# Four moves in a fused attention and feed-forward kernel: x's last transposes, a pair of output banks, one step up, and four idle matmuls

## The chip, the cores and the metric

The kernel runs on one core of a Trainium2 chip. Five engines work side by side, each through its own list of instructions in order: PE (matrix products and transposes, which write the PSUM banks), ACT (exponentials, Relu, copies), DVE (vector arithmetic and copies), POOL (masking of tiles, and issuing of loads) and SP (issuing of transfers). They wait for one another by semaphores. The metric is the device time of one execution in microseconds (us); lower is better.

## The reference, cut to what matters

Two parts follow one another. The first is attention for 4 batches, 8 heads, 768 tokens and 64 dimensions, in which each query sees only 6 of the 24 chunks of 32 keys, chosen by an upper bound (`ub`) from each chunk's smallest and largest key:

```python
ub = np.sum(np.maximum(q[:, :, :, None, :] * k_min[:, :, None, :, :], q[:, :, :, None, :] * k_max[:, :, None, :, :]), axis=-1)
top_chunks = np.argsort(ub, axis=-1)[..., -top_k:]
scores = scale * np.matmul(q, k.transpose(0, 1, 3, 2))
mask = sel & (pos[:, None] >= pos[None, :])
attn = np.exp(scores)      # of the masked scores, then divided by the row's sum
```

The second part takes the attention's result as x (3072 tokens of 512) through a feed-forward layer with 2048 hidden units:

```python
h = np.maximum(x @ w_in, 0.0)
return (h * h @ w_out).astype(np.float32)
```

## The kernel before, in words

**Slots.** The attention's work is cut into 32 slots, counted from 0. A slot is one batch, one half of its 768 tokens (384 queries) and one pair of heads. Four slots (four pairs) make a half batch, called hb; the order of the half batches is (batch 0, first half), (batch 1, first half), (batch 0, second half), (batch 1, second half), and so on. So slots 0 to 3 are hb 0, slot 4 (the fifth pair) opens hb 1, slot 8 opens hb 2, and slot 12 (the thirteenth slot) opens hb 3.

**Steps of a slot.** Each is a function, written below with the slot's number:
- P(s) transposes k and q of a slot on PE (L274: `tk`, `tq`). ACT and DVE copy them into `kq` (L300), ACT also makes q's positive and negative parts `qr` (L295), and DVE the chunk extrema `km` and `kbd` (L237, L240). From slot 12 on `qr` is made by DVE from transposes that the DMA did (L323, L324).
- U(s) forms the bounds `ub` on PE (L378 to L389), and DVE picks the six largest (L396) and marks the rest (L398: `chosen`, `nsel`).
- V(s) transposes the marks on PE (`qt`, L431 or L442), and DVE copies them beside q (L436, L447), so that the scores' own product adds a large negative number to chunks that were not chosen.
- E(s,h,n) makes scores `ps` of head h, part n (L460, and L468 for the triangular mask in slots 0 to 3), and ACT their exponentials `e` (L471). From slot 4 on POOL masks the diagonal blocks (L475).
- F(s) multiplies `e` with the values (`po`, L493), for both heads, and DVE divides by the sums (L502, L503), which gives a part of x.

**The feed-forward queue.** When the four pairs of a half batch have given x, it is transposed, on PE for some parts (`x_T`, L531, copied to `xT` by ACT or DVE at L537) and by DMA for others (L507). `push(hb)` then puts the half batch's steps into a queue: 16 steps up (`ffn_up`, L579: four matmuls for 128 hidden units, then Relu on ACT at L585 or L589 and a square on DVE) and 12 steps down (`ffn_down`, L602: four matmuls of 512 columns; four such steps (t,0) to (t,3) make the tile t of 128 output rows, which is then copied to `ob` and stored). `f1()` takes one step from the queue, and the loop over the slots places f1 calls between the attention's steps, by hand, up to a quota for each slot. This order is the order of each engine's list; nothing reorders it.

**PSUM.** Eight banks in four pools, handed out in turn: psS (3: scores, and some q or k transposes), psF (2, tag "ph": results of the steps up, transposes of x, early transposes of k), psY (1, tag "py": a tile of steps down, and some transposes) and psA (2: bounds, marks, `po`, and the idle matmuls). A tile that takes a bank waits until its last reader is done.

**Idle matmuls.** `busy(n)` (L685) issues n products of the identity with itself whose result nobody reads.

Of the kernel before, what the change touches and what calls it, by code (L numbers as in the profile page):

```python
# [30 lines left out]
ON_PE = 3  # L31
# [8 lines left out]
def kernel(  # L40
# [9 lines left out]
    nc = tc.nc  # L50
# [309 lines left out]
    def step_P(s):  # L360
        if s // NP >= ON_PE:
            relus(s)
            return
        step_T(s, *((S_, Y) if s == NP + 1 else (F, Y) if s < NP + 2 else
                    (Y, S_) if s < 2 * NP + 1 else (S_, A)))
        if s >= NP + 2 and s != 2 * NP + 1:
            step_T2(s)
# [168 lines left out]
    def x_copy(hb, g, u0, u1, copy):  # L536
        copy(xT_of(hb)[:, 2 * g + u0:2 * g + u1, :], pts[hb, g][:, u0:u1, :])  # L537
# [14 lines left out]
    def ffn_downs(hb, tail=False):  # L552
        py = {}
        order = [(t, c) for t in range(HT - tail) for c in range(4)]
        if hb == 0:

            order = [(0, 0), (0, 1), (1, 0), (1, 1), (0, 2), (1, 2), (0, 3), (1, 3)] + order[8:]
        return [lambda act, t=t, c=c: ffn_down(hb, py, t, c, act, tail) for t, c in order]

    def ffn_last(hb):  # L560
# [31 lines left out]

    def ffn_down(hb, py, t, c, act, tail):
        if c == 0:
            if hb == 0 and t == 1:
                py[t] = psF.tile([128, DM], F32, tag="ph", name="py")
            elif tail:
                py[t] = psS.tile([128, DM], F32, tag="ps", name="py")
            else:
                py[t] = psY.tile([128, DM], F32, tag="py", name="py")  # L600
        for f in range(4 * c, 4 * c + 4):
            nc.tensor.matmul(  # L602
                py[t], lhsT=h2[hb, f][:, 128 * t:128 * (t + 1)], rhs=w_out[:, f, :],
                start=(f == 0), stop=(f == NFI - 1))
        if c == 3:
            ob = late.tile([128, DM], F32, tag="ob", bufs=3, name="ob")
            if act:
                nc.scalar.copy(ob, py[t])  # L608
            else:
                nc.vector.tensor_copy(ob, py[t])  # L610
            r0 = S * ORDER[hb][0] + HB * ORDER[hb][1] + 128 * t
            nc.sync.dma_start(out[r0:r0 + 128, :], ob)
# [68 lines left out]
    def busy(n, pool=psA, tag="att"):  # L681

        idle = pool.tile([128, 128], F32, tag=tag, name="idle")
        for _ in range(n):
            nc.tensor.matmul(idle, lhsT=ident, rhs=ident, start=True, stop=True)  # L685
# [32 lines left out]
    late = ctx.enter_context(tc.tile_pool(name="late", bufs=2))  # L718
    for s in range(NP):
        last = s + 1 == NP  # L720
        if last:
            busy(4)
        if s:
            step_E(s, 0, 0)
            if not last:

                step_T(s + 2, F, Y, "k")
                extrema(s + 2, 0)
            step_E(s, 0, 1)
        step_E(s, 1, 0)  # L730
        if last:
            step_F(s - 1, 0)
            step_F(s - 1, 1)
        step_U(s + 1)
        if not last:
            busy(3)
            extrema(s + 2, 1)
            place(s + 1, "k", nc.scalar.copy)
        step_E(s, 1, 1)
        if last:  # L740
            x_T(0, 0, F)
            x_copy(0, 0, 0, 2, nc.scalar.copy)
            place(s + 1, "q", nc.scalar.copy)
            place(s + 1, "k", nc.scalar.copy, 1, 2)
            step_F(s, 0)
            step_F(s, 1)
            step_V(s + 1)
        else:
            step_T(s + 2, F, Y, "q")
            relus_T(s + 2)  # L750
            step_V(s + 1)
            if s:
                step_F(s - 1, 0)
                step_F(s - 1, 1)
            extrema(s + 2, 2)
            if s + 2 == NP:
                place(s + 2, "k", nc.vector.tensor_copy, 0, 1)
        go(s, 99)
    parts = []

    def k1():
        if parts:
            parts.pop(0)()

    for s, (b, half, p) in enumerate(slots):
        if s < NP:
            continue
        hb = s // NP
        nb = len(BANKS[half])
        hf = nb // 2  # L770
        quota = [((5, 5, 4, 4) if hb == 1 else (8, 5, 6, 7) if hb == 2 else (8, 6, 7, 7))[p]]
        for fn, *a in first.get(s, ()):
            fn(*a)
        if (hb == ON_PE - 1 and p == 2) or (ON_PE < hb < 2 * B - 1 and p == 0):
            parts.extend(step_K(hb + 1))

        def f1():
            if quota[0] and queue:
                quota[0] -= 1
                fill(1, True)  # L780

        if s == NP:
            for n in range(hf):
                step_E(s, 0, n)
            step_P(s + 1)
            relus_T(s + 1)
            x_T(0, 1, F)
            x_copy(0, 1, 0, 2, nc.vector.tensor_copy)
            push(0)
            extrema(s + 1)  # L790
            place(s + 1, "k", nc.vector.tensor_copy)
            place(s + 1, "q", nc.scalar.copy)
        if s == 2 * NP:
            for n in range(hf):
                step_E(s, 0, n)
            relus_T(s + 1)
            place(s + 1, "q", nc.scalar.copy)
            step_F(s - 1, 0)
            step_F(s - 1, 1)
            f1()  # L800
            x_T(1, 1, F, (1,))
            f1()
            extrema(s + 1)
            place(s + 1, "k", nc.vector.tensor_copy)
            put_off()
            x_copy(1, 1, 1, 2, nc.vector.tensor_copy)
            push(1)
        if p == 0 and hb > 2:
            step_F(s - 1, 0)
            step_F(s - 1, 1)  # L810
            put_off()
            push(hb - 1)
        else:
            f1()
        if s > NP and s != 2 * NP:
            for n in range(hf):
                step_E(s, 0, n)
        k1()
        f1()
        if p == 0 and hb > 2:  # L820
            f1()
            f1()
        if hb > 1 and s != 2 * NP:
            f1()
        if hb < ON_PE:
            go(s, 4 if s == 2 * NP else 2)
        for n in range(hf, nb):
            step_E(s, 0, n)
        if hb < ON_PE and p:
            k1()  # L830
        if s < NS - 2 or s + 1 == 3 * NP:
            step_U(s + (1 if hb < ON_PE else 2))
        if s == NP:
            put_off()
        if s + 1 == ON_PE * NP:
            put_off(2)
        if hb >= ON_PE and s < NS - 2:
            step_W(s + 2)
        if s == 2 * NP:

            for x in nsel:
                nc.vector.memset(
                    x[:, :, :, :, 1, :].rearrange("p i h j c -> p (i h j) c"), 0.0)
        late_f = half == 0 and hb > 2
        border = p == 0 and hb > 1
        if not border and not (late_f and p == NP - 1) and s + 1 != 2 * NP:
            f1()
        if p and s > NP:
            step_F(s - 1, 0)
            step_F(s - 1, 1)  # L850
        for fn, *a in by_sp.get(s, ()):
            fn(*a)
        if s + 1 == ON_PE * NP:
            step_P(s + 2)
            step_Q(s + 2)
        if half == 0 and not (late_f and p in (0, NP - 1)):
            f1()
        if hb < ON_PE and p:
            k1()
        for n in range(hf):  # L860
            step_E(s, 1, n)
            if border and half and n == 0:

                f1()
        if not (late_f and p == 0):
            f1()
        if s + 1 <= ON_PE * NP:
            step_V(s + 1)
        if s + 1 == ON_PE * NP:
            put_off(2)  # L870
        if hb == ON_PE and p == 0:
            parts.extend(step_K(hb + 1))
        k1()
        if hb < ON_PE:
            go(s, 99)
        for n in range(hf, nb):
            step_E(s, 1, n)
        if hb >= ON_PE:
            go(s, 99)
        k1()  # L880
        if hb == ON_PE - 1 or (hb == ON_PE and p):
            k1()
        if s + 1 < ON_PE * NP:
            step_P(s + 2)
            if s + 2 == ON_PE * NP:
                step_Q(s + 2)
        if s + 1 == ON_PE * NP:
            f1()
            step_U(s + 2)
            step_W(s + 2)  # L890
        if hb >= ON_PE or s + 1 == ON_PE * NP:
            if s + 3 < NS:
                step_P(s + 3)
                step_Q(s + 3)
        f1()
        if half == 0:
            f1()
        while quota[0] and queue:
            f1()
# [40 lines left out]
```

## Time and profile before

| | us |
|---|---|
| median of 3 runs | 266.37 (266.06 to 266.40) |
| the profiled execution | 266.18 |
| its span in the profile | 264.5 |

| engine | busy us | share of the span |
|---|---|---|
| PE | 253.7 | 96% |
| ACT | 178.4 | 67% |
| DVE | 162.5 | 61% |
| POOL | 91.1 | 34% |

The span runs from the first to the last instruction in the profile; 1.7 us of the execution lie around it. A row of the timeline gives start, length, engine, line of the kernel, operation, output<-inputs, shape and count; in brackets stands how long the engine was idle ahead of it and what ended the wait. Rows merge neighbouring instructions of one kind. The printed end of a PE row is modelled and overlaps the start of the next, so that the difference of two starts is the better measure of what PE spent. The granted clock of TensorE (PEclk) is 1.00 throughout.

### The profile page before, as it was taken

The page shows a single profiled execution, that of the slowest core. Times are in us where ns is not written, and L with a number is a line of the kernel's source. Part 1 is how long each engine was busy: PE and PEld are TensorE (multiplying, and loading weights), DVE is VectorE, ACT ScalarE, POOL GpSimd, SP SyncE. Part 2 cuts the span into 40 slices and gives each one's busy share as a digit, 9 for nine tenths or more (in the row PEclk, how much of TensorE's full clock was granted, in tenths as well). Part 3 has the DMA queues.
Part 4 walks back from the last instruction along what each step waited for, and adds up shares of the span by engine and source line. Part 5 has one row for each costly group of instructions (what it writes and reads, how often), then busy time and mean ns, then how long its engine had stood idle before and what let it go on. Part 6 is the DMA issues. An engine that isn't in the chain of part 4 may idle for free.

```text
span 264.5 us, 6559 instructions
## 1 busy us (share of the span) xinstructions
PE 253.7 (96%) x2402; PEld 157.4 (60%) x2428; DVE 162.5 (61%) x619; ACT 178.4 (67%) x399; POOL 91.1 (34%) x134
## 2 busy tenths in 40 slices
PE   7897999999999999999999999999999999999995
PEld 6575665556666566655565566745565666645543
DVE  6787998867986568566875566555863233424411
ACT  4898997698974787844685778835685788614500
POOL 8966445607902435225521543310120111000000
PEclk9999999999999999999999999999999999999999
DMA  7999999999994899999995999995642220111022
GB/s 140 162 194 189 206 219 184 135 182 112 155 158 90 141 164 156 133 158 153 184 144 119 147 157 130 212 126 127 123 99 64 72 45 17 58 40 41 0 82 79
DMA packets 116161, 33.69 MB, mean 127 GB/s; under 512 B 102560, under 2 KB 112576, under 8 KB 116128
## 3 DMA queue, kind: packets, MB, share of 16 engines
q0 software_dynamic: 65200, 13.83, 66.6%
q1 hardware_dynamic: 49984, 19.03, 37.7%
q10 hardware_dynamic: 944, 0.39, 0.6%
q8 instruction: 19, 0.31, 0.5%
q14 instruction: 14, 0.11, 0.1%
HBM read 27.26 MB, written 6.29 MB: 127 GB/s over the span
## 4 chain that ended last, share of the span: by engine, by line
PE 77%; DVE 8%; ACT 3%; issue 2%; ACTq 0%; DVEq 0%
PE py L602 28%; PE ph L579 26%; PE ps L460 11%; PE po L493 7%; DVE km L343 2%; ACT e L471 2%; PE ub L382 1%; PE py L567 1%; DVE km L237 1%; DVE kq L447 1%; DVE h L590 1%; DVE kq L300 1%; ACT ht L589 1%; PE tk L274 0%; ACT ob L608 0%
## 5 line engine op out<-in xcount | busy, mean ns | idle before, releaser
L471 ACT ACTIVATE e<-ps 128x512 bf16<-128x512 f32 x192 | 96.7, 550 | 18.9 <-PE ps L460 17.6
L579 PE MATMUL ph<-xT,w_in 128*128 128x384 bf16 x512 | 98.9, 325 | 0.4 <-DVE xT L537 0.4
L602 PE MATMUL py<-w_out,h 128*128 128x512 bf16 x342 | 82.7, 379 | 2.2 <-DVE kq L300 0.3
L590 DVE TENSOR_TENSOR h<-ht 128x384 bf16<-128x384 bf16 x114 | 41.8, 376 | 55.4 <-ACT ht L589 54.8
L475 POOL TENSOR_SCALAR_AFFINE_SELECT e<-e 128x384 bf16<-128x384 bf16 x56 | 30.1, 537 | 129.0 <-ACT e L471 128.8
L589 ACT ACTIVATE ht<-ph 128x384 bf16<-128x384 f32 x114 | 55.5, 500 | 26.8 <-PE ph L579 26.4
L579 PEld LDWEIGHTS <-w_in 128*128 128x128 bf16 x512 | 47.8, 97 | 30.7 <-issue 1.5
L460 PE MATMUL ps<-kq 96*128 96x384 bf16 (+2 forms) x320 | 57.9, 278 | 2.2 <-DVE kq L436 1.3
L602 PEld LDWEIGHTS <-h 128*128 128x128 bf16 x368 | 34.6, 97 | 35.6 <-issue 0.6
L460 PEld LDWEIGHTS <-kq 96*128 96x128 bf16 x320 | 26.4, 97 | 17.0 <-issue 2.6
L493 PEld LDWEIGHTS <-e 128*128 128x128 bf16 x672 | 25.2, 98 | 4.1 <-DVE x L503 0.4
L493 PE MATMUL po<-vn,e 128*128 128x65 bf16 x672 | 26.6, 194 | 0.3 <-DVE x L503 0.3
L608 ACT COPY ob<-py 128x512 f32<-128x512 f32 x18 | 10.5, 586 | 22.6 <-PE py L602 22.2
L396 DVE MAX8 m<-ub 128x8 f32<-128x16 f32 (+4 forms) x160 | 16.1, 166 | 15.6 <-PE ub L389 9.4
L503 DVE TENSOR_TENSOR x<-po,r 128x384 bf16<-128x384 f32 x32 | 17.8, 557 | 1.1
L237 DVE TENSOR_REDUCE km<-tk 128x12 bf16<-128x384 bf16 x24 | 12.5, 550 | 1.7 <-PE tk L274 1.4
L109 POOL DMA_DIRECT2D kn<-in_k_dram x15 | 13.3, 897 | 0.4 <-issue 0.3
L109 POOL DMA_DIRECT2D qn<-in_q_dram x15 | 13.3, 896 | 0.2
L125 POOL DMA_DIRECT2D vn<-in_v_dram x15 | 12.5, 842 | 2.0 <-DMA qn<-in_q_dram 1.3
L343 DVE TENSOR_TENSOR km<-km 128x384 bf16<-128x384 bf16 (+3 forms) x40 | 12.0, 300 | 1.1
L382 PEld LDWEIGHTS <-qr 128*128 128x128 bf16 x160 | 7.8, 96 | 4.8 <-DVE qr L323 1.7
L382 PE MATMUL ub<-kbd,qr 128*128 128x48 bf16 (+1 forms) x160 | 9.7, 180 | 1.0 <-DVE qr L323 0.5
(79 smaller groups left out, 193.3 us busy)
## 6 DMA issues: line engine op xcount, KB each, us to landing
out_dram<-ob SPq DMA_DIRECT2D x23, 256.0 KB, 2.4
w_out<-in_moe_w_out_dram POOLq DMA_DIRECT2D x2, 1024.0 KB, 18.2
kn<-in_k_dram POOLq DMA_DIRECT2D x15, 128.0 KB, 6.1
qn<-in_q_dram POOLq DMA_DIRECT2D x15, 128.0 KB, 5.9
kq<-kqT SPq DMA_DIRECT2D x10, 192.0 KB, 4.6
vn<-in_v_dram POOLq DMA_DIRECT2D x4, 384.0 KB, 7.8
vn<-in_v_dram POOLq DMA_DIRECT2D x9, 128.0 KB, 8.3
w_in<-in_moe_w_in_dram POOLq DMA_DIRECT2D x2, 512.0 KB, 9.0
```

Source lines behind the costliest of these rows:

```text
L109: nc.gpsimd.dma_start(out=nat_of(n, g)[:, DM * j:DM * j + DM].rearrange("p (h d) -> p h d", d=D), in_=rows(n, *ORDER[g], 0, H)[:, 128 * j: ...
L343: nc.vector.tensor_tensor(y, x[:, :, :, 0:m], x[:, :, :, m:2 * m], op=op)
L382: nc.tensor.matmul(ub[:, j - j0], lhsT=st[s]["qr"][:, w, 128 * j:128 * (j + 1)], rhs=kbds[b % 2][:, p, w, :, 0:ncs], start=bool(half) and ...
L460: nc.tensor.matmul(ps[:, at:at + 128 * m], lhsT=kqs[b % 2][0:KR, p, 2 * (j // HT), hh, 128 * (j % HT):128 * (j % HT + 1)], rhs=qc(s, hh)[: ...
L471: nc.scalar.activation(e[:, 512 * n + lo:512 * n + hi], ps[:, lo:hi], ACT.Exp, scale=float(scale))
L475: nc.gpsimd.affine_select(out=d, in_=d, compare_op=ALU.is_ge, fill=0.0, base=0, channel_multiplier=-1, pattern=[[0, 3], [1, 128]])
L493: nc.tensor.matmul(po[:, hh, i, :], lhsT=t["e"][hh][:, c:c + 128], rhs=vn[b % 2][:, 2 * p + hh, j, :], start=(j == 0), stop=(j == iq))
L503: nc.vector.tensor_mul(x[:, p].rearrange("p j (h d) -> p h j d", h=2), po[:, :, :, 0:D], r.to_broadcast([128, 2, HT, D]))
L579: nc.tensor.matmul(ph[:, 0:HB], lhsT=w_in[:, ki, 128 * f:128 * (f + 1)], rhs=xT[:, ki, :], start=(ki == 0), stop=(ki == NKI - 1))
L589: nc.scalar.activation(ht, ph[:, 0:HB], ACT.Relu)
L590: nc.vector.tensor_mul(h, ht, ht)
L602: nc.tensor.matmul(py[t], lhsT=h2[hb, f][:, 128 * t:128 * (t + 1)], rhs=w_out[:, f, :], start=(f == 0), stop=(f == NFI - 1))
```

## The change

Four edits, none of which changes what is computed:

1. In the last slot of hb 0 (slot 3) the four idle matmuls go, and F(2) runs ahead of E(3,1,0) instead of behind it.
2. In slot 4, P(5) and the transposes of x's second half of hb 0 (pairs 2 and 3) with their copy run ahead of E(4,0,0) instead of behind it.
3. Of hb 0's steps down, tile 0 takes a bank of psF and tile 1 that of psY, where it was the other way round, and (1,3) runs ahead of (0,3).
4. In slot 11, one step up runs ahead of U(12), and the one behind U(12) goes.

On PE's list the idle matmuls (eight rows with their weight loads) are all that goes. On ACT's list, slot 5's `qr` (L295) stands ahead of the exponential of E(4,0,0), and the two copies of the output tiles change places. DVE, POOL and SP keep their lists, but for which of the two tiles a store belongs to.

```diff
-            order = [(0, 0), (0, 1), (1, 0), (1, 1), (0, 2), (1, 2), (0, 3), (1, 3)] + order[8:]
+            order = [(0, 0), (0, 1), (1, 0), (1, 1), (0, 2), (1, 2), (1, 3), (0, 3)] + order[8:]
...
     def ffn_down(hb, py, t, c, act, tail):
         if c == 0:
-            if hb == 0 and t == 1:
+            if hb == 0 and t == 0:
                 py[t] = psF.tile([128, DM], F32, tag="ph", name="py")
...
     for s in range(NP):
         last = s + 1 == NP
-        if last:
-            busy(4)
...
             step_E(s, 0, 1)
-        step_E(s, 1, 0)
         if last:
             step_F(s - 1, 0)
             step_F(s - 1, 1)
+        step_E(s, 1, 0)
         step_U(s + 1)
...
         if s == NP:
+            step_P(s + 1)
+            x_T(0, 1, F)
+            x_copy(0, 1, 0, 2, nc.vector.tensor_copy)
+            relus_T(s + 1)
             for n in range(hf):
                 step_E(s, 0, n)
-            step_P(s + 1)
-            relus_T(s + 1)
-            x_T(0, 1, F)
-            x_copy(0, 1, 0, 2, nc.vector.tensor_copy)
             push(0)
...
+        if s + 1 == ON_PE * NP:
+            f1()
         if s < NS - 2 or s + 1 == 3 * NP:
             step_U(s + (1 if hb < ON_PE else 2))
...
-        if not border and not (late_f and p == NP - 1) and s + 1 != 2 * NP:
+        if not border and not (late_f and p == NP - 1) and s + 1 not in (2 * NP, 3 * NP):
             f1()
```

## The prediction

> **What bounds the kernel.** I read the page's first part and its chain, then the windows, then what PE waited for, then the timeline engine by engine around the three places that the change touches.
>
> ```profile
> span 264.5 us, 6559 instructions
> ...
> PE 253.7 (96%) x2402; PEld 157.4 (60%) x2428; DVE 162.5 (61%) x619; ACT 178.4 (67%) x399; POOL 91.1 (34%) x134
> ...
> PE 77%; DVE 8%; ACT 3%; issue 2%; ACTq 0%; DVEq 0%
> ```
> ```profile
> core 0: us, PE busy (x) PEld busy (x) DVE busy (x) ACT busy (x) POOL busy (x), PEclk, DMA share, GB/s
> 20.00:30.00 10.00, 8.39 (x117) 5.64 (x116) 7.69 (x30) 8.77 (x21) 5.39 (x8) 1.00 1.51 196
> 30.00:44.00 14.00, 13.36 (x161) 8.64 (x156) 13.36 (x46) 12.89 (x33) 8.32 (x12) 1.00 1.27 209
> ...
> 84.00:120.00 36.00, 35.66 (x333) 22.04 (x336) 21.62 (x85) 24.90 (x54) 13.12 (x18) 1.00 1.33 146
> ```
> ```profile
> PE ps L460 <- DVE kq L447: 1.0, 1, 1.0
> ```
>
> PE is the bound: the chain is 77% PE, and from 84 to 120 us PE is idle for 36.00 - 35.66 = 0.34 us. From 20 to 30 us it is idle for 1.61 us, and the waits name its longest stop; the others stand in brackets in the rows below. A stop of PE that goes away in the first 84 us is time off the end, unless another engine or a transfer takes the stop's place. From 30 to 44 us DVE is as full as PE (13.36 of 14.00 us), so there both must move.
>
> **The opening, 19 to 27 us.** Slots count from 0, so the fifth pair is slot 4.
>
> ```profile
> 19.42 0.38 PE L685 MATMUL idle<-ident 128*128 128x128 bf16 x4 [0.27 <-DVE kq L436]
> 19.64 0.39 PE L460 MATMUL ps<-kq 96*128 96x384 bf16 x2
> ...
> 20.14 0.38 PE L460 MATMUL ps<-kq 96*128 96x384 bf16 x2
> ...
> 20.48 0.54 PE L493 MATMUL po<-vn,e 128*128 128x65 bf16 x12
> 20.85 0.18 PE L378 MATMUL ub<-cmask,ident 128*128 128x48 bf16 x1
> ...
> 22.44 0.30 PE L442 MATMUL qt<-ident,chosen 128*64 128x128 bf16 x2
> 23.72 0.38 PE L460 MATMUL ps<-kq 96*128 96x384 bf16 x2 [0.98 <-DVE kq L447]
> 24.03 0.37 PE L274 MATMUL tk<-ident,kn 96*64 96x96 bf16 x8
> 24.23 0.36 PE L274 MATMUL tq<-ident,qn 96*64 96x96 bf16 x8
> 24.52 0.51 PE L531 MATMUL pt<-ident,x 128*128 128x128 bf16 x6
> 24.87 0.49 PE L579 MATMUL ph<-xT,w_in 128*128 128x384 bf16 x2
> 25.73 1.14 PE L579 MATMUL ph<-xT,w_in 128*128 128x384 bf16 x6 [0.38 <-DVE xT L537]
> ...
> 26.98 1.46 PE L579 MATMUL ph<-xT,w_in 128*128 128x384 bf16 x8
> ```
> ```profile
> 20.23 1.64 ACT L471 ACTIVATE e<-ps 128x512 bf16<-128x512 f32 x4 [0.28 <-PE ps L468]
> 21.73 0.83 ACT L537 COPY xT<-pt 128x768 bf16<-128x768 bf16 x1
> 22.41 0.99 ACT L300 COPY kq<-tq 64x384 bf16<-64x384 bf16 x2
> ...
> 24.20 0.60 ACT L471 ACTIVATE e<-ps 128x512 bf16<-128x512 f32 x1 [0.42 <-PE ps L460]
> 24.69 0.65 ACT L295 ACTIVATE qr<-tq 128x256 bf16<-128x256 bf16 x2
> 25.22 0.96 ACT L300 COPY kq<-tq 64x384 bf16<-64x384 bf16 x2
> 26.26 0.49 ACT L585 ACTIVATE h<-ph 128x384 bf16<-128x384 f32 x1
> ```
>
> Starts of neighbouring rows give what a step takes on PE; the printed lengths overlap. The four idle matmuls take 19.64 - 19.42 = 0.22 us. They wait for the same DVE copy (L436) as the scores after them, so without them E(3,0,0) starts at 19.42. F(2) takes 20.85 - 20.48 = 0.37 us; it now runs ahead of E(3,1,0) and needs only exponentials of slot 2, which were finished before ACT went idle ahead of 20.23.
>
> What this does to ACT: the first exponential comes 20.23 - 19.64 = 0.59 us after its scores start. E(3,1,0) now starts at 19.42 + 0.50 (for E(3,0,0) and E(3,0,1), as from 19.64 to 20.14, where E(3,1,0) stood) + 0.37 = 20.29, and its exponential at 20.88. Half of the block (21.73 - 20.23 = 1.50) follows from there, so the xT copy starts at 21.63 instead of 21.73. ACT gains only 0.1 us.
>
> That matters, because slot 5's q transposes (tq) write the bank that ACT's two copies of slot 4's q (L300) must empty first. Before, the scores stood ahead of them and hid that; now the whole PE queue behind V(4) (tq, x's transposes, E(4,0,0), the steps up) waits for it. The copies end at 22.41 + 0.99 - 0.10 = 23.30, so tq can start at about 23.35. Then tq takes 0.29 (24.52 - 24.23) and x's transposes 0.35 (24.87 - 24.52): E(4,0,0) starts at 23.99, later than its 23.72 of before, takes 0.31, and the steps up start at 24.30 instead of 24.87. DVE's copies of slot 4's masks, which held E(4,0,0) for 0.98 us, are done by then: they follow V(4), which is no later than 22.44, and ended by 23.72 before.
>
> ```profile
> 29.87 0.36 DVE L590 TENSOR_TENSOR h<-ht 128x384 bf16<-128x384 bf16 x1 [0.28 <-ACT ht L589]
> ```
>
> The third matmul of the first step up waits for the copy of x's last transposes; it came 25.73 - 24.52 = 1.21 us after they started, so now at 23.64 + 1.21 = 24.85: 0.88 us earlier. But the third step up needs the bank of the first, which ACT empties after e(4,0,0) and the two q copies of slot 5. E(4,0,0) at 23.99 gives its exponential at 24.47 (0.48 later, as 24.20 to 23.72); with 0.49 until the next one starts (24.69 - 24.20) and 0.96 for the copies, the first step's Relu starts at about 25.92 and ends at 26.41, and the third step up starts at 26.46 instead of 26.98. I take this 0.52, not 0.88. The stretch from 30 us on is paced by DVE as well, but DVE enters it idle (0.28 us before 29.87, waiting for ACT on the fifth step up), so it moves with PE. Bounds: nothing if tq gets its bank 0.5 us later than 23.35, a loss beyond that; at most 1.0, if all of the stop at 23.72 goes.
>
> **The banks.**
>
> ```profile
> 43.77 1.04 PE L602 MATMUL py<-w_out,h 128*128 128x512 bf16 x3 [0.32 <-DVE kq L300]
> ```
> ```profile
> 42.93 0.49 ACT L585 ACTIVATE h<-ph 128x384 bf16<-128x384 f32 x1
> ```
>
> The first step down took the bank from which DVE still copied slot 8's k, and PE stopped for 0.32 us. It now takes a bank of the steps up, freed when ACT ends the fifteenth step's Relu at 42.93 + 0.49 = 43.42: it starts at 43.47, 0.30 earlier. Tile 1 takes the other bank three steps later, long after DVE's copy. Swapping (0,3) and (1,3), and with them their copies on ACT and their output DMAs on SP's queue, costs nothing: the tile in the bank that tile 2 needs still ends one step (four matmuls) ahead of tile 2's first. Bounds 0 (ACT late by 0.3) to 0.32.
>
> **The step up in slot 11.**
>
> ```profile
> 74.65 0.55 PE L460 MATMUL ps<-kq 96*128 96x128 bf16 x3
> 75.70 0.47 PE L382 MATMUL ub<-kbd,qr 128*128 128x48 bf16 x6 [0.50 <-DVE qr L323]
> 76.03 0.81 PE L579 MATMUL ph<-xT,w_in 128*128 128x384 bf16 x4
> 76.68 1.12 PE L493 MATMUL po<-vn,e 128*128 128x65 bf16 x30
> ```
> ```profile
> 74.56 0.89 ACT L585 ACTIVATE h<-ph 128x384 bf16<-128x384 f32 x2
> ```
>
> The scores end at 74.65 + 0.55 = 75.20, but printed ends overlap the next start by some 0.17 (24.03 + 0.37 against 24.23), so PE is free at about 75.03. The step up needs a bank that the first of the two Relus frees at 74.56 + 0.49 = 75.05 (0.49 by the row of 42.93). With 0.05 for the signal it runs from 75.10 for 76.68 - 76.03 = 0.65 us to 75.75. Then the bounds run without a stop, since qr was there at 75.70: they took 76.03 - 75.70 = 0.33 while the second half of qr came late; by their columns (seven matmuls of up to 48, where a transpose of 128 takes 0.058) 0.15 is enough, and I take 0.22. F(10) starts at 75.97 instead of 76.68: 0.71 less. Nobody waits longer for U(12): its result comes at 76.0 either way. Bounds: 0.50 (the stop alone) to 0.72; 0.33 if the bank comes only with the second Relu at 75.45.
>
> **Sum.** 0.52 + 0.30 + 0.71 = 1.53 us, against the profiled execution: 264.5 of span and 1.7 around it, 266.18; it is 0.2 below the runs' median of 266.37. 266.18 - 1.53 = 264.65, from the median 264.84; I say 264.8.
>
> Does a transfer take over? The nearest is the last half of w_in, which the ninth step up needs:
>
> ```profile
> 19.84 0.76 POOL L631 DMA_DIRECT2D w_in<-in_moe_w_in_dram  x1
> ```
> ```profile
> w_in<-in_moe_w_in_dram POOLq DMA_DIRECT2D x1, 1024.0 KB, 12.0
> ```
> ```profile
> 33.37 0.81 PE L579 MATMUL ph<-xT,w_in 128*128 128x384 bf16 x4
> ```
>
> It lands at 19.84 + 12.0 = 31.8; the step moves from 33.37 to 32.85. One microsecond is left.
>
> **Rivals.** (a) The opening gives nothing: tq's bank frees at 23.9 or later, or the third step up keeps waiting for ACT. For it: ACT is busy 8.77 of 10 us there, the stage's fullest engine. Then 0.30 + 0.71 = 1.01: 265.3. (b) ACT keeps up and 0.88 to 1.0 arrives: about 1.95, 264.4. (c) The edits move PE but the time goes back later, to a load or to DVE's full stretch from 30 to 44 us: 266.0 to 266.4. Against it: after 84 us PE hardly waits, and w_in has a microsecond.
>
> (d) Slower: PE drops to a low rate after the new stop.
>
> ```profile
> 1.43 3.17 PE L685 MATMUL idle<-ident 128*128 128x128 bf16 x28 [1.43 <-POOL ident masks.py:199]
> ```
>
> At the start 28 idle matmuls take 3.17 us, 0.11 each; at 19.42 four take 0.22, 0.055 each: PE begins at half rate. If the stop after V(4), with the idle matmuls gone, sent it back there for as long as at the start (3.17 us), 1.6 us would be lost, which cancels the sum; for two such stretches, 3.2 us lost, 267.9. It decides from a stop longer than the 0.98 us ahead of 23.72, after which six transposes still ran in 0.35 (0.058 each, full rate). The new stop is 23.35 less V(4)'s end (22.2 to 22.6) and less 0.2 of k transposes, at most 0.95; so I give it little. The Trainium skill's page "TensorE: Matmul & The Clock Gate" (HAM oscillation) warns against gaps of over about 3.4 us; by that rule nothing drops here, and the 0.98 us row agrees as far as it goes.
>
> **How the numbers follow.** Forecast (264.5 to 265.1) 0.58; (a) and parts of it 0.18; (b) 0.10; (c) 0.08; (d) 0.06. The range 264.0 to 265.9 holds forecast, (a) and (b): with every upper bound 1.0 + 0.32 + 0.72 = 2.04 goes (264.3), with the least of slot 11 alone 0.50 (265.9). A measurement here tells about 0.2% from no change: faster is below 265.84, slower above 266.90. Faster 0.86, same 0.08 (all of (c)), slower 0.06.
>
> **What would show it.** No row of idle matmuls at 19.4; tq with a stop ahead of it that names ACT's L300; E(4,0,0) behind x's transposes near 24.0; the step up's copy L537 at 24.2; the third step up near 26.5. The first step down waiting for ACT L585 instead of DVE L300, 0.8 earlier in all. In slot 11 no stop ahead of U(12), and F(10) about 1.5 earlier than 76.68. From there every row stands 1.5 earlier to the end. I am wrong if tq starts after 23.9, if a DMA appears among PE's waits, or if the lead at 84 us is gone at 240.

## The result, and the profile after

The changed kernel takes 265.21 us (median of 9 executions, 264.96 to 265.51), the kernel before 266.33 beside it (9, 266.06 to 267.69): a ratio of 0.9953, with a 95% interval of 0.9939 to 0.9966. It is faster by 1.1 us; 264.8 was predicted, 1.5 us faster. The profiled execution took 265.17 with a span of 263.5, 1.0 us below that of before.

The page's first part and the chain of the kernel after:

```profile
span 263.5 us, 6549 instructions
...
PE 253.6 (96%) x2398; PEld 157.4 (60%) x2424; DVE 162.9 (62%) x619; ACT 178.4 (68%) x399; POOL 91.0 (35%) x134
...
PE 88%; ACT 5%; DVE 4%; issue 2%; POOL 0%; ACTq 0%; POOLq 0%
```

Its windows, in the columns of the prediction's:

```profile
20.00:30.00 10.00, 8.48 (x117) 5.82 (x114) 8.34 (x30) 9.04 (x22) 6.00 (x9) 1.00 1.49 196
30.00:44.00 14.00, 13.60 (x158) 8.78 (x155) 13.38 (x47) 12.89 (x33) 8.34 (x12) 1.00 1.27 209
84.00:120.00 36.00, 35.66 (x333) 22.02 (x335) 22.65 (x89) 24.90 (x54) 13.64 (x18) 1.00 1.36 155
```

PE is still the bound, and its idle time from 20 to 30 us fell only from 1.61 to 1.52 us: the opening has new stops in place of the old one. What PE waited for in the kernel after (us in total, times, longest):

```profile
PE tq L274 <- ACT kq L300: 0.8, 1, 0.8
PE ph L579 <- ACT h L585: 0.5, 1, 0.5
```

The 0.98 us on DVE's mask copies (L447), the 0.32 ahead of the first step down and the 0.50 ahead of U(12) are gone; 0.8 and 0.5 us on ACT have come. PE's timeline in the three places:

```profile
19.55 0.38 PE L460 MATMUL ps<-kq 96*128 96x384 bf16 x2 [0.27 <-ACT e L471]
...
22.17 0.30 PE L442 MATMUL qt<-ident,chosen 128*64 128x128 bf16 x2
22.31 0.36 PE L274 MATMUL tk<-ident,kn 96*64 96x96 bf16 x8
23.47 0.37 PE L274 MATMUL tq<-ident,qn 96*64 96x96 bf16 x8 [0.80 <-ACT kq L300]
23.77 0.51 PE L531 MATMUL pt<-ident,x 128*128 128x128 bf16 x6
24.12 0.38 PE L460 MATMUL ps<-kq 96*128 96x384 bf16 x2
24.34 0.49 PE L579 MATMUL ph<-xT,w_in 128*128 128x384 bf16 x2
24.99 1.14 PE L579 MATMUL ph<-xT,w_in 128*128 128x384 bf16 x6 [0.16 <-DVE xT L537]
...
26.92 1.46 PE L579 MATMUL ph<-xT,w_in 128*128 128x384 bf16 x8 [0.53 <-ACT h L585]
```
```profile
43.41 1.02 PE L602 MATMUL py<-w_out,h 128*128 128x512 bf16 x3
```
```profile
74.75 0.81 PE L579 MATMUL ph<-xT,w_in 128*128 128x384 bf16 x4
75.40 0.40 PE L382 MATMUL ub<-kbd,qr 128*128 128x48 bf16 x6
75.64 0.17 PE L389 MATMUL ub<-cmask,ident 128*128 128x24 bf16 x1
75.67 1.12 PE L493 MATMUL po<-vn,e 128*128 128x65 bf16 x30
```

Start by start against before: the third step up leads by 0.06 us (26.98 to 26.92), the first step down by 0.36 (43.77 to 43.41), F(10) by 1.01 (76.68 to 75.67), and PE's last product still ends 1.01 earlier (261.62 to 260.62). One correction: executions of one kernel start up to 0.3 us apart because their first loads land differently. In the profiled execution of after, the last bounds of slot 1, which no edit touches, start 0.12 later than before. So the edits brought 0.18 in the opening, 0.30 at the banks and 0.65 in slot 11, 1.13 in all. All gains named below are corrected in this way; "the opening" is from those bounds to the fifth step up (28.50 before).

ACT's timeline shows where the opening went:

```profile
22.45 0.97 ACT L300 COPY kq<-tq 64x384 bf16<-64x384 bf16 x2
23.32 0.47 ACT L300 COPY kq<-tk 64x384 bf16<-64x384 bf16 x1
23.88 0.66 ACT L295 ACTIVATE qr<-tq 128x256 bf16<-128x256 bf16 x2
24.91 0.60 ACT L471 ACTIVATE e<-ps 128x512 bf16<-128x512 f32 x1 [0.37 <-ACT qr L295]
25.41 0.95 ACT L300 COPY kq<-tq 64x384 bf16<-64x384 bf16 x2
26.38 0.87 ACT L585 ACTIVATE h<-ph 128x384 bf16<-128x384 f32 x2
```

The exponential of E(4,0,0) starts at 24.91, 0.79 after its scores (24.12). In the trace the row of its wait for the scores (a semaphore) ended at 24.56, and ACT had ended the Relus (L295) at 24.54, yet ACT stood still for 0.35 us more; before, the same exponential started 0.04 us after the end of its wait. Below, "after its semaphore" is counted from the end of that row. Everything behind the exponential on ACT is later by that, and so is the third step up.

### The profile page after: what moved, and what is told of

Read it like the earlier page. It is cut to its first block, busy times and chain, and to the rows that moved or that the text cites. A ratio compares the mean times of both kernels' runs of the same rounds, so it can differ in the third digit from the quotient of the medians.

```text
span 263.5 us, 6549 instructions
## 1 busy us (share of the span) xinstructions
PE 253.6 (96%) x2398; PEld 157.4 (60%) x2424; DVE 162.9 (62%) x619; ACT 178.4 (68%) x399; POOL 91.0 (35%) x134
## 4 chain that ended last, share of the span: by engine, by line
PE 88%; ACT 5%; DVE 4%; issue 2%; POOL 0%; ACTq 0%; POOLq 0%
PE ph L579 29%; PE py L602 29%; PE ps L460 13%; PE po L493 8%; ACT e L471 2%; PE ub L382 2%; PE idle L685 2%; PE py L567 1%; PE tk L274 1%; ACT kq L300 1%; DVE km L343 1%; PE qt L431 1%; DVE km L237 1%; PE qt L442 1%; ACT qr L295 1%
## 5 line engine op out<-in xcount | busy, mean ns | idle before, releaser
L503 DVE TENSOR_TENSOR x<-po,r 128x384 bf16<-128x384 f32 x32 | 17.8, 558 | 1.1
```

Of the source, the lines that this page charges most:

```text
L503: nc.vector.tensor_mul(x[:, p].rearrange("p j (h d) -> p h j d", h=2), po[:, :, :, 0:D], r.to_broadcast([128, 2, HT, D]))
```

## The experiments

### Each edit alone

```diff
 first: before with edit 1 alone (no busy(4); F(2) ahead of E(3,1,0))
 xfirst: before with edit 2 alone (P(5), x_T, x_copy, relus_T ahead of E(4,0,n))
 bank: before with edit 3 alone
-            order = [..., (0, 2), (1, 2), (0, 3), (1, 3)] + order[8:]
+            order = [..., (0, 2), (1, 2), (1, 3), (0, 3)] + order[8:]
-            if hb == 0 and t == 1:
+            if hb == 0 and t == 0:
 stepup: before with edit 4 alone
+        if s + 1 == ON_PE * NP:
+            f1()
-        if not border and not (late_f and p == NP - 1) and s + 1 != 2 * NP:
+        if not border and not (late_f and p == NP - 1) and s + 1 not in (2 * NP, 3 * NP):
```

> Edit 1 alone: the four idle matmuls go and F(2) runs ahead of E(3,1,0); slot 4 keeps the order of before. Theory A (ACT paces the opening: its copies of slot 4's q come only 0.1 us earlier, and what they hold comes no earlier than that): 0.1 us off, ratio 0.9996. Rival B (DVE's copies of slot 4's marks pace it, and they follow V(4), which the changed kernel has 0.27 us earlier): E(4,0,0) and all behind it 0.2 to 0.3 us earlier, ratio 0.999.

> Edit 2 alone: slot 5's k and q transposes and x's last transposes ahead of E(4,0,0). Theory A (tq waits for ACT's copies of slot 4's q, and the third step up waits for ACT's first Relu, which comes behind e(4,0,0) and slot 5's q copies): a stop of about 0.9 us ahead of tq, one of about 0.5 ahead of the third step up, and at most 0.1 us off in all. Rival C (the 0.37 us for which ACT stood still ahead of e(4,0,0) in the changed kernel was an accident of that execution): the stop ahead of the third step up is 0.2 us and 0.4 us are off, ratio 0.9985.

> Edit 3 alone: tile 0 of hb 0's steps down in a bank of psF, tile 1 in psY, (1,3) ahead of (0,3). By its step in the prediction 0.30 us off: the first step down starts 0.3 us earlier, and nothing behind it stops. Ratio 0.9989. Rival: the lead is gone before slot 8, ratio 1.000.

> Edit 4 alone: a step up ahead of U(12). By its step in the prediction 0.71 us off, by the changed kernel's trace 0.65: no stop ahead of U(12), F(10) 0.65 us earlier, kept to the end. Ratio 0.9975. Rival: part of it goes to a later wait, ratio 0.999 or more.

Measured beside the kernel before at 266.30: first 266.16 (12 executions; ratio 1.0006, 0.9990 to 1.0021), xfirst 266.20 (11; 0.9991, 0.9976 to 1.0005), bank 266.07 (11; 0.9995, 0.9983 to 1.0007), stepup 265.90 (11; 0.9994, 0.9981 to 1.0006). (The recorded ratio is not the quotient of the two medians, which is 0.9995 for first and 0.9985 for stepup.) One edit alone is too small for these intervals to tell it from no change; the traces resolve them. Bank gains 0.30 between the fifth step up and the first step down and keeps it. Stepup gains 0.65 in slot 11 and keeps it. Its executions show less: the interval does not reach the expected 0.9975, and the medians differ by 0.4 us, or 0.5 among the executions that kept their clock (8 of its 11, 265.8; 32 of 36 of before, 266.3). Where the rest of the 0.65 is, no run shows. Xfirst gains 0.09 in the opening, with a stop of ACT like the one in after:

```profile
24.77 0.60 ACT L471 ACTIVATE e<-ps 128x512 bf16<-128x512 f32 x1 [0.38 <-ACT qr L295]
```

First is the surprise. Its E(4,0,0) started 0.33 us earlier than before, which is more than either theory said. Yet its profiled execution lost 1.26 us in the opening. Its windows (the last three columns are granted clock, DMA share, GB/s) and PE's timeline:

```profile
23.00:25.00 2.00, 1.63 (x26) 1.10 (x27) 0.74 (x3) 1.81 (x6) 0.38 (x1) 1.00 2.21 165
25.00:27.00 2.00, 1.81 (x7) 0.90 (x7) 1.95 (x6) 1.11 (x3) 1.14 (x2) 0.58 1.41 204
27.00:29.00 2.00, 2.00 (x14) 1.10 (x13) 1.74 (x8) 0.94 (x3) 1.44 (x2) 0.56 1.12 215
29.00:31.00 2.00, 2.00 (x24) 1.14 (x24) 0.91 (x4) 1.80 (x5) 0.00 (x0) 1.00 1.24 198
```
```profile
23.18 0.38 PE L460 MATMUL ps<-kq 96*128 96x384 bf16 x2 [1.05 <-ACT kq L300]
...
25.19 1.96 PE L579 MATMUL ph<-xT,w_in 128*128 128x384 bf16 x6 [0.38 <-DVE xT L537]
...
27.35 2.13 PE L579 MATMUL ph<-xT,w_in 128*128 128x384 bf16 x8
```

By the clock's own record in the trace PE had half its clock from 25.34 to 28.75, 3.41 us (the windows give 2 x (0.42 + 0.44) / 0.5 = 3.44): a matmul of a step up took 0.32 us instead of 0.16. The stop ahead of E(4,0,0) had grown from 0.98 to 1.05 us. The granted clock of its executions shows that this happens in some and not in others: 4 of the 12 had a mean clock of 0.994 (267.2 to 267.3 us), the rest 265.5 to 266.3.

### The change without edit 2

```diff
 no_xfirst: before with edits 1, 3 and 4
```

> Edits 1, 3 and 4, without edit 2 (slot 4 in the order of before). If edit 2 is what gives the opening its gain, this is slower than the changed kernel, 0.9958 to 0.9965. If edit 2 gives nothing, or costs, beside edit 1, since both stops it makes are ACT's, it is as fast or faster: 0.9950 to 0.9955.

265.19 us (9; before 266.35 in this batch; ratio 0.9951, 0.9929 to 0.9973): not to be told from after. Its profiled execution kept the full clock in the opening, which gained 0.33 us, more than the 0.18 of after with edit 2 as well. E(4,0,0) waits for ACT's copies there, as in first, and its exponential started 0.04 after its semaphore:

```profile
23.67 0.38 PE L460 MATMUL ps<-kq 96*128 96x384 bf16 x2 [1.05 <-ACT kq L300]
```

So by the traces edit 1 carries the opening, and the stop of ACT that came with edit 2 eats more than edit 2 brings.

### What stands ahead of the stop on ACT, and behind it

```diff
 relu_late: after, slot 5's Relus (L295) behind the exponential of E(4,0,0)
-            relus_T(s + 1)
             for n in range(hf):
                 step_E(s, 0, n)
+            relus_T(s + 1)
 q_late: after, slot 5's two q copies behind the Relus of the first two steps up
-            place(s + 1, "q", nc.scalar.copy)
...
         f1()
+        if s == NP:
+            place(s + 1, "q", nc.scalar.copy)
 tq_bank: after, slot 5's q transposes in a bank of psA instead of psY
-        step_T(s, *((S_, Y) if s == NP + 1 else ...
+        step_T(s, *((S_, A) if s == NP + 1 else ...
```

> The changed kernel, with slot 5's two Relus of q (L295) behind the exponential of E(4,0,0) on ACT, where they were before. If the 0.37 us stop of ACT ahead of e(4,0,0) comes from the Relus standing directly ahead of it, it is gone here, the first step's Relu comes 0.3 us earlier and 0.3 us are off: 0.9942. If it is an accident of one execution, it is absent here and in the other kernels with edit 2 alike. If ACT's amount of work paces the stage, nothing changes: 0.9953.

> The changed kernel, with slot 5's two q copies (L300, 0.96 us on ACT) behind the first two steps up's Relus instead of ahead of them. Theory A (the third step up waits for the first Relu, which stands behind these copies): the stop of 0.53 us ahead of the third step up goes, and 0.5 us are off beyond the changed kernel, ratio 0.9935. Rival D (from 27 us on DVE paces the stage, whatever PE does): the stop goes, and another of the same size comes ahead of bounds or scores before 44 us; ratio 0.9953.

> The changed kernel, with slot 5's q transposes in a bank of psA instead of psY, so that they don't wait for ACT's copies of slot 4's q. The stop of 0.80 us ahead of tq shrinks to about 0.4 (that bank is freed by DVE's product L503 at about 23.1), and E(4,0,0) starts 0.4 us earlier. If that stop paces the opening, 0.4 us are off (0.9938). If the Relu of the first step up does, behind ACT's fixed list, less than 0.2 is off, as ACT is busy until 23.8 with the copies: 0.9946 to 0.9953.

Relu_late: 265.52 (12; ratio 0.9966, 0.9947 to 0.9984). No stop ahead of the exponential (0.04 from its semaphore), but the Relus of `qr` now come between it and the Relu of the first step up; the third step up waits longer, and the opening gains nothing (-0.04):

```profile
27.26 1.46 PE L579 MATMUL ph<-xT,w_in 128*128 128x384 bf16 x8 [0.76 <-ACT h L585]
```

Q_late: 265.03 (12; 0.9945, 0.9925 to 0.9966), opening 0.30. The third step up no longer waits, as the chain through the q copies says. But 0.12 us are gained beyond after and not 0.5, because the next wait stands two steps up later. It is a wait for ACT, not for DVE as rival D had it:

```profile
24.61 1.14 PE L579 MATMUL ph<-xT,w_in 128*128 128x384 bf16 x6 [0.15 <-DVE xT L537]
...
25.86 1.46 PE L579 MATMUL ph<-xT,w_in 128*128 128x384 bf16 x8
27.16 0.38 PE L460 MATMUL ps<-kq 96*128 96x384 bf16 x2
27.96 0.81 PE L579 MATMUL ph<-xT,w_in 128*128 128x384 bf16 x4 [0.42 <-ACT ht L589]
```

Tq_bank: 264.69 (6; 0.9928, 0.9908 to 0.9948), opening 0.52. The q transposes wait 0.45 instead of 0.80 (now for DVE, L503), so E(4,0,0)'s semaphore comes while ACT still runs the Relus, and the late exponential (0.38 after its semaphore) starts only 0.09 after their end. The third step up still waits 0.56 for ACT. What the other bank brings is thus mostly that it hides the stop of ACT: after_shift (below) removes the stop, leaves the bank as it was, and gains 0.50.

### Is it the place in ACT's list?

In after, xfirst, q_late and tq_bank the late exponential is record 63 of ACT's list in the trace (counted from 0, waits included), in before, no_xfirst, relu_late and the others, where it is prompt, record 61. Either the place in the list makes it late (theory P), or what surrounds it (theory R). One instruction more at the very start of the list, a second exponential of one column, moves the place and leaves the work as it is:

```diff
 after_shift: after with one more; relu_late_shift: relu_late with two more; best_shift: best with one more
-    nc.scalar.activation(warm, ident[:, 0:1], ACT.Exp)
+    nc.scalar.activation(warm, ident[:, 0:1], ACT.Exp); nc.scalar.activation(warm, ident[:, 0:1], ACT.Exp)
 best: after with the edits of tq_bank and q_late together
```

> The changed kernel with one more tiny exponential (128 numbers) at the start of ACT's list, so that every later ACT instruction stands one place further down its list; the work is otherwise the same. In the changed kernel ACT starts e(4,0,0) 0.37 us after its Relus' end, with its scores long there. Theory P (the stop belongs to a place in ACT's list, as where the sequencer has to fetch the next piece of code): it is gone, e(4,0,0) starts about 0.06 us after the Relus, the third step up 0.3 us earlier, 0.3 us off: 0.9942. Theory R (it belongs to an exponential right behind two Relus of q with a wait for PE between them): it stays at 0.37 us, ratio 0.9953.

> The kernel with slot 5's Relus behind e(4,0,0), with two more tiny exponentials at the start, which puts e(4,0,0) at the place in ACT's list that it has in the changed kernel. There it started 0.06 us after its scores were signalled. Theory P: a stop of some 0.35 us ahead of e(4,0,0) appears. Theory R: none; 0.06 us as before, ratio 0.9966.

> The changed kernel with both of the edits tried before: slot 5's q transposes in a bank of psA, and its q copies behind the first two steps up's Relus. If both stops of the opening are then short, about 1.0 us is off in the opening (0.5 of it beyond the changed kernel's own): 0.992 to 0.993. If the later stop that the late copies made (0.42 us ahead of the fifth step up, waiting for ACT) comes back in full, it is as the kernel with psA's bank alone: 0.9928 to 0.9935.

> The same, with one more tiny exponential at the start of ACT's list. Theory P: the stop ahead of e(4,0,0) goes and up to 0.3 us more are off, 0.9915 to 0.992. Theory R: as without it.

ACT's timeline in after_shift, where the exponential is record 64, and in relu_late_shift, where it is record 63:

```profile
24.03 0.66 ACT L295 ACTIVATE qr<-tq 128x256 bf16<-128x256 bf16 x2
24.75 0.60 ACT L471 ACTIVATE e<-ps 128x512 bf16<-128x512 f32 x1
```
```profile
23.32 0.47 ACT L300 COPY kq<-tk 64x384 bf16<-64x384 bf16 x1
24.92 0.60 ACT L471 ACTIVATE e<-ps 128x512 bf16<-128x512 f32 x1 [1.14 <-PE ps L460]
```

In after_shift the stop is gone (0.04 from the semaphore) with the same Relus ahead; in relu_late_shift it has come (0.38) with no Relus ahead. Theory P holds, R falls:

| kernel | record of the exponential | end of its wait to start, us | gain in the opening, us | median, us (executions) | ratio to before, 95% interval |
|---|---|---|---|---|---|
| after | 63 | 0.35 | 0.18 | 265.21 (9) | 0.9953 (0.9939 to 0.9966) |
| after_shift | 64 | 0.04 | 0.50 | 264.89 (6) | 0.9929 (0.9902 to 0.9956) |
| relu_late | 61 | 0.04 | -0.04 | 265.52 (12) | 0.9966 (0.9947 to 0.9984) |
| relu_late_shift | 63 | 0.38 | -0.37 | 265.73 (11) | 0.9953 (0.9927 to 0.9979) |
| tq_bank | 63 | 0.38 | 0.52 | 264.69 (6) | 0.9928 (0.9908 to 0.9948) |
| best | 63 | 0.36 | 0.64 | 264.73 (6) | 0.9921 (0.9898 to 0.9944) |
| best_shift | 64 | 0.17 | 0.65 | 264.71 (6) | 0.9919 (0.9896 to 0.9943) |

Over all profiles it is the same: 0.35 to 0.38 us in the six kernels with the exponential at 63, 0.04 at 61 or 64 (0.17 in best_shift, where ACT was still in the Relus). In tq_bank and best ACT was in the Relus as well for the first 0.29 us of the 0.38 and 0.36; there the late exponential starts 0.09 and 0.08 after the printed end of the Relus, in best_shift 0.11 ahead of it. The medians alone would not show 0.3 us: the intervals of after and after_shift overlap, and the two relu_late kernels cannot be told apart by theirs. In best a load of q also landed late and PE waited for it at 9.5 us; its opening is therefore counted from E(3,0,0), plus the 0.22 of the idle matmuls. Best_shift gains no more than best, against the 0.3 us that theory P allowed: there the late exponential costs little, and the wait of q_late comes behind it in both:

```profile
27.60 0.81 PE L579 MATMUL ph<-xT,w_in 128*128 128x384 bf16 x4 [0.42 <-ACT ht L589]
```

Tq_bank, best and best_shift beat the kernel before by 1.6 to 1.9 us against their own runs of it, and after, whose own gain is 1.1, by some 0.5 to 0.75; which of the three is best is not settled.

## Why the prediction was right or wrong

**The opening: the mechanism right, a term mis-sized, 0.18 for 0.52.** The chain went as told: tq waits for ACT's two q copies (23.47 against 23.35, of which 0.12 is the later start), E(4,0,0) follows at 24.12 against 23.99, and the third step up waits for ACT's first Relu. The step that failed is "E(4,0,0) at 23.99 gives its exponential at 24.47 (0.48 later, as 24.20 to 23.72)": it came 0.79 later. The price was taken from a row where the exponential stood at another place of ACT's list. In after_shift the distance is 24.75 - 24.27 = 0.48, and the opening gains 0.50: with the stop away, the term is right.

**The banks: right in size.** 0.30 for 0.30, alone and in after. The sign that was named, a wait for ACT (L585), did not appear: no wait stands ahead of 43.41, so the bank was free when PE came.

**The step up in slot 11: right within 0.06 by the traces.** With the lead of 0.36 it was due at 75.10 - 0.36 = 74.74 and started at 74.75. The bounds took 75.67 - 75.40 = 0.27 where 0.22 was taken.

**The sum.** 1.53 less 0.34 for the opening and 0.06 for the bounds is 1.13; less the later start of 0.12 it is the 1.01 of the two profiles. The medians give 1.12. The result lies between the forecast and rival (a), inside the range.

**The rivals.** (a) held in part: tq started well before 23.9, but the third step up does keep waiting for ACT, 0.53 us, of which 0.22 are left without the stop (after_shift). (b) fell: 0.88 was not to be had, as ACT's chain is the limit even in best (0.64). (c) fell: the lead of 1.01 at 75.67 is there at the end, and from 84 to 120 us PE is busy 35.66 us as before.

(d) did not happen in after, whose stop is 0.80, but the mechanism is real. In first its price was 1.26 + 0.33 = 1.59 us (against the opening of no_xfirst), where 1.6 was estimated from the idle matmuls. The prediction took a stop of 0.98 us as safe, from one trace. With that stop the kernel before had a mean clock of 0.981 to 0.994 in 12 of 78 executions; where in them the clock fell is not on record, so that the 0.98 is not shown to be safe. A stop of 1.05 came with the drop in first and without one in the trace of no_xfirst, so length alone does not decide it. Relu_late_shift says the same: it has stops of 0.80 and 1.10 us, and none of its 11 executions lost the clock. The Trainium skill's page "TensorE: Matmul & The Clock Gate" (HAM oscillation) sets the limit at idle gaps of about 3.4 us. The half clock in first lasted 3.41 us, but PE's longest stop in the 3.41 us ahead of it was 1.05, with another of 0.38: here the measurement decides, and far shorter stops can be enough.

## What to carry to other kernels

When a step is moved, follow the queue that it moves into to the next engine: here the whole gain of the opening was set by ACT's chain, not by the PE stop that went. A gain from one more edit need not be that edit's own: the other bank of tq_bank gained 0.34 us beyond after, but moving the list by one place (after_shift) gained nearly as much, 0.32, with the old bank. Judge edits of 0.3 us by the traces, against a point ahead of the edit, since start-up alone moves by as much and medians hide it. Where one instruction starts late with its wait done and its engine free, move it by one place in the list before looking for a cause in its neighbours.

## What the runs showed of the hardware

- Two places of ACT's list were late. The exponential of E(4,0,0) started 0.35 to 0.38 us after its semaphore when it stood at record 63, directly behind its wait, and 0.04 at record 61 or 64. Other instructions at record 63 followed without a gap, while ACT was still busy with the ones ahead. The second place is record 447, which is 384, or six times 64, behind 63. The exponential there starts 0.32 us after the end of its wait and 0.55 after the Relu ahead of it, in before and after alike; in after_shift, where it stands elsewhere, it starts 0.39 after that Relu. PE loses nothing by it. Before, then after_shift:

```profile
185.98 0.49 ACT L589 ACTIVATE ht<-ph 128x384 bf16<-128x384 f32 x1
186.53 0.60 ACT L471 ACTIVATE e<-ps 128x512 bf16<-128x512 f32 x1
```
```profile
184.80 0.49 ACT L589 ACTIVATE ht<-ph 128x384 bf16<-128x384 f32 x1
185.19 0.59 ACT L471 ACTIVATE e<-ps 128x512 bf16<-128x512 f32 x1
```

  At the records between (127, 191, 255, 319 and 383) the traces of before and after show no stop: ACT is busy there, or has waited long for its input. So a period of 64 fits but is not shown, and what happens at these places (a fetch of instructions would fit) no run here shows.
- PE had half its clock for one stretch of 3.41 us in the trace of first. The full-clock records that end within the traces are whole numbers of such stretches long: 20.48 us (6) ahead of the drop in first, 256.00 (75) or 259.41 (76) elsewhere. Which stops fall into one stretch may decide. In first the last stretch ahead of the drop (21.93 to 25.34) held both stops, 1.05 and 0.38 us, and PE was busy for 1.98 us of it. In no_xfirst the same two stops fell into two stretches (20.38 to 23.79 and 23.79 to 27.21, PE busy for 2.33 and 3.04), and the clock stayed. In before one stretch (22.57 to 25.98) held stops of 0.98 and 0.38, with PE busy for 2.05, and the clock stayed. This fits the one drop that was traced; it was not tested.
- A mean clock of 0.98 to 0.995 was seen in 23 of 121 executions of the kernels without edit 2 (before, first, bank, stepup, no_xfirst), and in 2 of 79 of those with it, where the stop after V(4) is 0.80 us in after. So the loss is rarer with edit 2; where in an execution it lay was seen in first alone.
